# A gated linear recurrence with a two-layer MLP on one core: the order table of all five engines replaced

## The chip, the cores and the metric

The kernel runs on one core of a Trainium2 chip. The metric is device time in microseconds (us) of one execution, as a median over runs. The engines are named as in the profile: PE (TensorE; its weight loads are listed apart as PEld), DVE (VectorE), ACT (ScalarE), POOL (GpSimd) and SP (SyncE, which here only issues DMAs). PSUM has eight banks, which PE writes and DVE and ACT read.

## The reference, cut to what matters

```python
# q, k, v, a_re, a_im: (4, 8, 768, 48) = batch, heads, steps, head_dim
mag = sqrt(a_re*a_re + a_im*a_im)
scale = minimum(mag, 0.999) / (mag + 1e-6)
ar, ai = a_re*scale, a_im*scale
for t in range(768):                       # per batch and head; S is 48 x 48, complex
    S_re, S_im = ar*S_re - ai*S_im + outer(k[t], v[t]), ar*S_im + ai*S_re   # ar, ai at step t, by row of S
    y[t] = q[t] @ S_re
x = y with the heads side by side          # (4, 768, 384)
xn = (x - mean(x)) / sqrt(var(x) + 1e-6) * g_ln
out = x + maximum(xn @ w_ch1, 0) @ w_ch2   # 384 -> 1536 -> 384
```

A complex number a at each step and channel turns and shrinks the state; k times v is added; q reads the real part. A layer norm and an MLP with a residual follow.

## The kernel before

**Tiling.** The 768 steps of a batch are cut in chunks of 128. Two chunks make a *pair*, so there are 12 pairs P (0 to 11, three for each of the four batches) and 24 chunks n. Pair 0 is done in two halves of four heads each (names with .0 and .1 behind the pair number), all other pairs in one piece.

**The steps of a pair.** Loads a_re, a_im, q, k and v (tiles are, aim, q, k, vf; L449 and L408). ACT takes ln(a_re) (L452) and 1/a_re as Exp (L454); DVE or POOL form the ratio r = a_im/a_re; its square r2 is made by DVE, POOL or ACT (L462 on ACT), and ACT takes u = ln(1 + r2) (L466). DVE makes l = u/2 + ln(a_re) and caps it (the capped one is called lc). PE sums the log decays along the steps with a triangular matrix (dec, L481) and ACT makes from these sums e and en, their Exp with plus and minus sign (L485). ACT takes the angle th = arctan(r), PE sums it into phases (ph, L506 to L514; in turns, read as 16-bit integers), ACT reads sine and cosine from these (pairs 0 to 2 over a quarter turn that PE adds, qt; the others over an absolute value, abs, that ACT (L549) or DVE makes), and the last phase is carried to the next pair (car, on ACT L524, or DVE). Then the products: ke = k en, qe = q e (two halves each, m = 0 and 1), ks = ke times cosine and times sine, qs likewise (L293 is the helper line of all these products; the last digit of ks.P.i.a is 0 for the cosine, 1 for the sine). So each pair after pair 0 has two ks and two qs products, 128x768 each, on DVE or POOL.

**Attention.** For each chunk, ks and qs are transposed: on PE into PSUM (kT, qT, eight transposes each, L612) with a copy out by ACT (L288) or DVE (L290), the tiles ksT and qsT; or, with no PE work, by a DMA transpose on SP's queue (L617). am = ksT times qsT (L635), masked to atm by DVE; y = atm v + qsT G (L685, L688), copied to x by ACT or DVE; G is the state, from gm (L659, L663).

**MLP.** x is transposed by PE (xtr, L706) and copied to xT, or transposed by DMA (L712). mm1 multiplies by w1b (L740; 36 matmuls a pair, in three groups gi of two parts), relu goes to h (ACT L757 or DVE L759), and mm2 multiplies by w2b (L772; three parts for each chunk, part j needing the group j of h and the weight piece wl.3+j). bn makes mean and variance, rstd is 1/sqrt of the variance (POOL, L725 and L727; on ACT a Ln and an Exp, L722), oa and ot scale and add x (L778, L785, L788), st stores (L795). The weights come by six loads on POOL's queue: wl.0 to wl.2 fill w1b (L368), wl.3 to wl.5 fill w2b (L370). g_ln and the mean are folded into w1b at the start (wp, wc).

ACT holds one table set at a time. Ln and Exp need the one (tab.log), Arctan and Sin the other (tab.trig), and each change is a load on L810. In the start PE runs filler matmuls (warm, L805).

**What sets the order.** Nothing is scheduled while it runs or by the compiler: a text, PLAN (L39), lists every operation as *name:engine and PSUM bank*, and each engine's row is the order of its tokens in this text. Letters: P is PE, A ACT, V DVE, G POOL, S SP's queue. A DMA on A is issued from ACT's queue, in ACT's row. An '@' and a name behind a token is an added wait: this operation starts only after the named one, even though it doesn't use its result. All other waits follow from the data and from buffers: each tile has a ring of two to ten buffers, and a step that writes a buffer waits for the readers of what was in it.

```python
aim.0.0:A are.0.0:S pickf:V tab.log.0:A ln.0.0:A iv.0.0:A are.1.0:S gln:S ue:G cmean:G uth:V r.0.0:V are.0.1:S one:G
...
ke.7.0.0:G ks.7.0.0:G lc.8.0:V mm2.11.1:P6 mm2.11.2:P6 u.9.0:A ln.10.0:A y.12:P5 x.12:A5 mm2.10.1:P0 k.8.0:S l.9.0:V
```

A buffer's number in a row of an engine is the pair, or the chunk, modulo the ring: ks1 is ks of pair 1, 4, 7 or 10 (three buffers), ksT0 and ksT1 are ksT of chunks 20 and 21 in pair 10 (four buffers).

Of the kernel before, what the change touches and what calls it, by code (L numbers as in the profile page):

```python
# [69 lines left out]
ph.3.0:P0 atm.2:V4 car.3.0:V0 u.3.0:A xtr.3:P2 xT.3:V2 y.2:P6 x.2:A6 abs.3.0:V0 r.4.0:G mm1.0.2.0:P4 tab.trig.5:A  # L70
sin.3.0:A0 G.3:V7 xtr.2:P2 xT.2:V2 k.3.1:S are.6.0:S bn.2:V mm1.0.2.1:P4 mm1.1.1.0:P2 are.7.0:S mm1.1.2.1:P6
mm1.1.1.1:P2 bn.3:V cos.3.0:A relu.0.2:V4 bn.1:V pad.ks.2:G@ks.1.0.1 mm1.1.2.0:P6 relu.1.2:V6 mm1.1.0.1:P4 l.3.0:V
are.5.0:S ke.2.0.1:G@ks.1.0.1 ks.2.0.0:V th.4.0:A mm1.1.0.0:P4 mm2.0.0:P0 lc.3.0:V relu.1.1:A2 q.4.0:S qs.2.0.0:V
aim.6.0:S mm2.1.0:P3 mm2.1.1:P3 r2.4.0:G@ks.1.0.0 tab.log.6:A u.4.0:A ks.2.0.1:V vf.3.0:S aim.5.0:S relu.1.0:A4
l.4.0:V v.2:A rstd.1:A dec.3.0:P6 en.3.0:A6 k.4.0:S e.3.0:A6 mm2.0.1:P0 qs.2.0.1:V mm2.1.2:P3 kT.5:P5 kT.4:P1 rstd.0:G
vf.3.1:S q.5.1:S oa.1:A3 lc.4.0:V dec.4.0:P6 ksT.5:A5 qe.3.0.0:V qe.3.0.1:V qs.3.0.1:V en.4.0:A6 qs.3.0.0:V mm2.2.0:P2
mm2.0.2:P0 ot.0:V0 qT.4:P3 e.4.0:A6 mm2.2.1:P2 mm2.2.2:P2 qsT.4:V3 ke.3.0.1:G@qs.3.0.0 ln.6.0:A ke.3.0.0:V ks.3.0.1:G
k.4.1:S ph.4.0:P6 ln.5.0:A st.0:S iv.5.0:A iv.6.0:A ot.2:V2 ksT.4:V1 car.4.0:V6 ks.3.0.0:G@ke.3.0.0 dps.3:P4 qT.7:P2
qsT.7:A2 dps.4:P5 q.4.1:S decc.3:V4 r.6.0:G@ke.3.0.0 qT.5:P0 r.5.0:G@ke.3.0.0 r2.5.0:G decc.4:V5 abs.4.0:A6 qT.6:P3
q.5.0:S qsT.5:V0 am.4:P4 atm.4:V4 gm.4:P0 qsT.6:V3 tab.trig.7:A cos.4.0:A mm2.3.0:P1 kT.6:P2 G.4:A0 mm2.3.1:P1  # L80
v.3:G@ke.3.0.0 ksT.6:V2 am.5:P4 are.9.0:S k.5.0:S atm.5:V4 sin.4.0:A6 kT.7:P3 ksT.7:V3 y.4:P0 mm2.3.2:P1 vf.4.0:S
ot.3:V1 th.5.0:A x.4:A0 qe.4.0.0:G y.5:P5 x.5:V5 am.6:P6 ot.1:G atm.6:V6 qe.4.0.1:G@ke.3.0.0 th.6.0:A aim.7.0:S
vf.4.1:S am.7:P2 xtr.4:P1 k.6.0:S atm.7:V2 xT.4:A1 xtr.5:P0 xT.5:A0 ph.5.0:P4 abs.5.0:A4 sin.5.0:A4 gm.6:P0 cos.5.0:A
mm1.2.1.0:P6 G.6:V0 ke.4.0.1:G@qs.3.0.0 y.6:P1 x.6:V1 mm1.2.1.1:P6 relu.2.1:V6 y.7:P5 x.7:A5 bn.7:V xtr.6:P1
ke.4.0.0:G@qs.3.0.0 xT.6:A1 k.5.1:S mm1.2.2.0:P2 r2.6.0:A xtr.7:P5 xT.7:V5 ks.4.0.1:V q.6.0:S qs.4.0.1:V mm1.2.0.1:P6
mm1.2.0.0:P6 relu.2.0:V6 gm.7:P0 G.7:V0 mm1.3.0.1:P4 tab.log.8:A u.5.0:A l.5.0:V mm1.2.2.1:P2 relu.2.2:A2 mm1.3.0.0:P4
relu.3.0:A4 bn.5:V u.6.0:A lc.5.0:V are.8.0:S ks.4.0.0:G@qs.4.0.1 ksT.8:S mm1.3.1.0:P6 mm1.3.1.1:P6 mm1.3.2.1:P2
dec.5.0:P4 mm1.3.2.0:P2 relu.3.1:A6 v.4:V mm2.5.0:P6 qs.4.0.0:V qT.8:P7 l.6.0:V kT.9:P0 lc.6.0:V e.5.0:A4
qe.5.0.1:G@l.6.0 en.5.0:A4 dec.6.0:P4 bn.4:V relu.3.2:V2 ln.7.0:A ksT.9:V0 iv.7.0:A rstd.2:A en.6.0:A4 mm2.5.1:P6
# [5 lines left out]
xtr.9:P5 xT.9:A5 xtr.8:P1 xT.8:A1 aim.10.0:S rstd.3:G mm2.6.1:P0 ke.6.0.1:V ke.6.0.0:G mm2.6.2:P0 oa.7:A4 ph.7.0:P2
abs.7.0:A2 mm1.4.0.0:P6 sin.7.0:A2 car.7.0:A2 q.7.1:S ot.6:V0 ks.5.0.1:V ks.6.0.0:V mm1.4.1.1:P4 qsT.10:S mm1.4.1.0:P4
bn.8:V mm1.4.0.1:P6 qT.11:P1 relu.4.1:A4 tab.log.10:A ln.9.0:A qsT.11:V1 v.5:G@ks.5.0.1 mm1.4.2.1:P2 mm1.4.2.0:P2
relu.4.2:A2 dec.7.0:P4 en.7.0:A4 qs.6.0.1:G@ks.5.0.1 kT.11:P1 relu.4.0:V6 ot.7:G@lc.7.0 st.4:S e.7.0:A4 mm2.9.0:P7
# [743 lines left out]
```

## Time and profile before

| | |
|---|---|
| median of 3 runs | 190.76 us (189.49 to 191.31) |
| span of the profiled execution | 187.1 us |
| PE busy | 176.4 us, 94% |
| DVE busy | 153.7 us, 82% |
| ACT busy | 160.0 us, 86%, of it 24.4 in 19 table loads |
| POOL busy | 111.1 us, 59% |
| DMA moved | 37.39 MB, 200 GB/s in the mean |

The span runs from the first to the last instruction of the profiled execution; the runs' times hold what lies around it too. A row of a group names the line, the engine, the operation, the tiles (out <- in) with their shape, and the count; behind the bar stand the busy time and the mean of one in ns, and behind the next bar the idle time just ahead of these instructions on their engine with what ended it. A row of the chain of waits gives the start and the length of a stretch of the chain, in us from the span's start, and whose work it was. A row of the timeline gives start and length of one instruction, and in brackets the wait ahead of it with what ended it. A busy PE is not a PE at its best pace: its time holds short waits between matmuls too.

### The profile page before, as it was taken

The numbers are of one execution on the slowest core, as the hardware profiler recorded it, in microseconds if no ns is written. First come the engines' busy times: TensorE is split into PE (matmuls) and PEld (weight loads), VectorE is DVE, ScalarE is ACT, GpSimd is POOL, SyncE is SP. The second block draws the span as 40 slices with busy tenths as digits, with TensorE's granted clock in tenths as the row PEclk, the third lists the DMA queues.
The fourth block names the chain that finished last, engine by engine and source line by source line (L and its number), as shares of the span: only waits on it lengthen the run. The fifth ranks groups of instructions, "written<-read, shape, count | busy, mean of one in ns | idle before, by whom it ended". The sixth has DMA issues, their size and how long they took to land.

```text
span 187.1 us, 5110 instructions
## 1 busy us (share of the span) xinstructions
PE 176.4 (94%) x2025; PEld 135.1 (72%) x2027; DVE 153.7 (82%) x275; ACT 160.0 (86%) x228; POOL 111.1 (59%) x130
## 2 busy tenths in 40 slices
PE   5978898999999999999999999999999998999993
PEld 3756565787767789866687696878867866778772
DVE  1479999999989999999979989899879888866332
ACT  3889999999999989999999999998999897274560
POOL 3328699589207996288176692365879759420600
PEclk9999999999999999999999999999999999999999
DMA  5999999999999999699999997999999969996122
GB/s 148 291 256 227 223 260 189 207 206 194 233 261 239 219 221 191 128 203 309 204 155 238 256 265 92 185 247 169 216 175 215 203 144 229 210 199 173 40 90 84
DMA packets 132439, 37.39 MB, mean 200 GB/s; under 512 B 126528, under 2 KB 132416, under 8 KB 132416
## 3 DMA queue, kind: packets, MB, share of 16 engines
q1 hardware_dynamic: 123040, 32.45, 83.9%
q0 software_dynamic: 2784, 2.36, 8.2%
q10 hardware_dynamic: 6592, 2.26, 4.7%
q8 instruction: 16, 0.26, 0.6%
q14 instruction: 7, 0.06, 0.1%
HBM read 28.31 MB, written 4.72 MB: 177 GB/s over the span
## 4 chain that ended last, share of the span: by engine, by line
PE 71%; DVE 10%; DMA 6%; ACT 4%; POOL 3%; SPq 2%; issue 2%; DVEq 0%; POOLq 0%
PE banks L772 25%; PE banks L740 21%; PE banks L635 5%; PE banks L612 4%; PE banks L506 4%; PE banks L481 4%; DMA aim<-in_a_im_dram 3%; PE banks L685 2%; DMA qsT<-qs 2%; PE banks L706 2%; PE banks L688 2%; DMA are<-in_a_re_dram 2%; PE banks L663 2%; SPq L408 1%; DVE r L293 1%
## 5 line engine op out<-in xcount | busy, mean ns | idle before, releaser
L772 PE MATMUL banks<-w2b,h 128*128 128x384 bf16 (+1 forms) x300 | 53.8, 319 | 0.0
L740 PE MATMUL banks<-xT,w1b 128*128 128x256 bf16 x432 | 51.4, 272 | 0.2 <-DVE xT L290 0.2
L740 PEld LDWEIGHTS <-w1b 128*128 128x128 bf16 x432 | 41.3, 98 | 6.3 <-issue 0.4
L772 PEld LDWEIGHTS <-h 128*128 128x128 bf16 x300 | 27.1, 97 | 13.3
L293 DVE TENSOR_TENSOR atm<-banks,mask 128x1024 bf16<-128x1024 f32 x24 | 28.8, 1219 | 5.1 <-PE banks L635 5.0
L757 ACT ACTIVATE h<-banks 128x1024 bf16<-128x1024 f32 (+1 forms) x24 | 23.8, 1003 | 5.3 <-PE banks L740 5.1
L293 POOL TENSOR_TENSOR qe<-q,e 128x384 bf16<-128x384 f32 x19 | 17.5, 929 | 15.7 <-ACT e L485 9.1
L810 ACT ACT_TABLE_LOAD x19 | 24.4, 1283 | 1.7 <-PEq L826 1.3
L293 POOL TENSOR_TENSOR ke<-k,en 128x384 bf16<-128x384 f32 x16 | 14.8, 939 | 7.5 <-DVE qs L293 6.8
L759 DVE TENSOR_SCALAR h<-banks 128x1024 bf16<-128x1024 f32 (+1 forms) x13 | 15.2, 1169 | 3.6 <-PE banks L740 3.6
L805 PE MATMUL banks<-u_e 128*128 128x256 f16 x111 | 15.5, 297 | 2.2 <-POOL u_e L322 2.2
L635 PE MATMUL banks<-qsT,ksT 128*128 128x128 bf16 x192 | 14.1, 219 | 1.0 <-DMA qsT<-qs 0.7
L805 PEld LDWEIGHTS <-u_e 128*128 128x128 f16 x111 | 11.5, 106 | 4.5 <-POOL u_e L322 1.9
L293 POOL TENSOR_TENSOR r<-aim,are 128x768 f16<-128x768 f32 x7 | 12.6, 1811 | 3.0 <-ACT are L454 3.0
L635 PEld LDWEIGHTS <-ksT 128*128 128x128 bf16 x192 | 11.9, 98 | 2.5 <-issue 1.1
L293 POOL TENSOR_TENSOR qs<-qe,trig 128x768 bf16<-128x768 bf16 (+1 forms) x8 | 12.6, 1576 | 1.6 <-DVE qe L293 0.9
L470 DVE SCALAR_TENSOR_TENSOR l<-r,w 128x768 f16<-128x768 f16 (+1 forms) x13 | 12.3, 949 | 1.3 <-ACT r L466 1.1
L785 POOL TENSOR_TENSOR ot<-ot,x 128x384 f32<-128x384 f32 x11 | 10.5, 966 | 4.6 <-ACT ot L778 4.3
L698 DVE BATCH_NORM_STATS2 stats<-x 128x6 f32<-128x384 bf16 x24 | 13.1, 548 | 0.0
L288 ACT CAST x<-banks 128x384 bf16<-128x384 f32 x19 | 8.8, 478 | 5.0 <-PE banks L688 4.5
L293 POOL TENSOR_TENSOR ks<-ke,trig 128x768 bf16<-128x768 bf16 (+1 forms) x7 | 10.7, 1539 | 2.8 <-DVE qs L293 1.6
L685 PE MATMUL banks<-v,atm 128*128 128x48 bf16 x192 | 11.9, 183 | 0.0
(101 smaller groups left out, 380.4 us busy)
## 6 DMA issues: line engine op xcount, KB each, us to landing
q<-in_q_dram SPq DMA_DIRECT2D x24, 192.0 KB, 4.7
k<-in_k_dram SPq DMA_DIRECT2D x24, 192.0 KB, 4.5
...
```

The source lines that it names most:

```text
L293: {"DVE": nc.vector, "POOL": nc.gpsimd}[eng(name)].tensor_tensor(**kw)
L470: nc.vector.scalar_tensor_tensor(out=S_("l"), in0=S_("r2"), scalar=0.5, in1=S_("w"), op0=ALU.mult, op1=ALU.add)
L635: nc.tensor.matmul(ps[:, h], lhsT=T("ksT", n)[:, h], rhs=T("qsT", n)[:, h], start=True, stop=True)
L685: nc.tensor.matmul(ps[:, h], lhsT=T("atm", n)[:, h], rhs=T("v", P)[:, c, h], start=True, stop=nfirst)
L698: nc.vector.bn_stats(out=T("stats", n), in_=T("x", n))
L740: nc.tensor.matmul(ps[:, jj], lhsT=w1b[:, dc, ts(gi * JG + jj, C)], rhs=T("xT", P)[:, dc].rearrange("p c t -> p (c t)"), start=(dc == 0), ...
L757: act(out=dst, in_=src, func=AF.Relu)
L759: nc.vector.tensor_scalar(out=dst, in0=src, scalar1=0.0, scalar2=None, op0=ALU.max)
L772: nc.tensor.matmul(bank(own)[:, 0:w], lhsT=T("h", P)[:, j, ts(c, C)], rhs=w2b[:, j, es], start=(j == 0), stop=(j == NJ - 1))
L785: nc.gpsimd.tensor_tensor(out=T("ot", n)[:, es], in0=T("ot", n)[:, es], in1=T("x", n)[:, es], op=ALU.add)
L805: g.add(f"warm.{i}", lambda i=i: nc.tensor.matmul(bank(f"warm.{i}")[:, 0:256], lhsT=u_e[:, 0, 0], rhs=u_e[:, 1].rearrange("p j t -> p (j t ...
L810: g.add(f"tab.{nm}.{i}", lambda tab=tab: nc.scalar.preload_act_table_set(tab))
```

## The change

Only the text PLAN differs. The same operations are computed, 1,137 tokens where there were 1,136: one table load less on ACT (tab.log.18, the 19th), and two more groups of eight PE transposes, kT.10 and qT.17, since ksT.10 and qsT.17 were DMA transposes on SP and are now copied out of PSUM, by DVE and by ACT. DMA transposes that remain: 11 of ks, 11 of qs and 1 of x, where there were 12, 12 and 1. All five rows have a new order, many PSUM banks are renumbered, and there are 51 added waits where there were 49.

Steps that change engine, counted over the whole program:

| step | moves |
|---|---|
| ks | 10 from DVE to POOL, 3 from POOL to DVE |
| qs | 4 and 4 |
| ke, qe | ke 3 DVE to POOL, 4 back; qe 4 DVE to POOL, 7 back |
| abs, car | 3 and 4 from DVE to ACT |
| x, xT | x 8 from ACT to DVE, 1 back; xT 11 from ACT to DVE, 4 back |
| ksT, qsT copies | ksT 1 ACT to DVE, 1 DVE to ACT; qsT 3 DVE to ACT, 2 ACT to DVE |
| relu, G, r | relu 4 ACT to DVE, 5 back; G 3 and 3; r 1 and 1 |
| r2 | both halves of pair 0 and 3 pairs from ACT to DVE, 1 DVE to ACT, and 4 moves from or to POOL |
| rstd | 4 ACT to POOL, 2 POOL to ACT |
| v | one each from POOL to ACT and to DVE, 2 from DVE to POOL |
| DMA issues | vf 5 and a_im 1 from ACT's queue to SP's, q 1 back; stores 6 from ACT's to SP's, 4 back |

The first and a late piece of the table, as the diff has them:

```diff
-aim.0.0:A are.0.0:S pickf:V tab.log.0:A ln.0.0:A iv.0.0:A are.1.0:S gln:S ue:G cmean:G uth:V r.0.0:V are.0.1:S one:G
+are.0.1:S tab.log.0:A ue:G aim.0.1:S uth:V warm.0:P0 warm.1:P0 warm.2:P0 are.0.0:S ln.0.1:A are.1.0:S car0.1:G
+aim.0.0:S warm.3:P0 iv.0.1:A warm.4:P0 r.0.1:V warm.5:P0 ln.0.0:A warm.6:P0 aim.1.0:S pad.ks.0:G iv.0.0:A r2.0.1:V
```

SP's row begins with a_re and a_im of pair 0's second half, a_re of its first half and of pair 1, a_im of the first half and of pair 1, and k of pair 0; before, it began with a_re of the first half, of pair 1 and of the second half, a_im of the second half (that of the first half was ACT's to issue) and q of pair 0.

The weight load wl.5 stood right behind wl.4 on POOL; it now stands behind r.4 and waits for DVE's lc.3 (wl.5:G@lc.3.0). In the change of tables ahead of pair 3's phases, xT.2 stands behind the load on ACT now. Of the vf loads, vf.6.0 stands on SP behind the DMA transpose qsT.12. Of the twelve ks and qs products of pairs 9, 10 and 11, POOL has eight (three with a wait on a relu or an xT), where it had four. Both stores of the last chunk are issued by SP, where one was ACT's.

ACT, from its first table load on: before, w0, are0 and r20 are pair 0 (two halves), w1, are1 and r21 pair 1; L462 is a Square, L466 the Ln behind it, L485 an Exp of the decay sums.

```order
L810 ACT_TABLE_LOAD
L452 ACTIVATE w0_82<-are0_64 128x384
L454 ACTIVATE are0_64<-w0_82 128x384
L462 ACTIVATE r20_87<-r0_84 128x384
L466 ACTIVATE r20_87<-r20_87 128x384
L452 ACTIVATE w1_83<-are1_65 128x768
L452 ACTIVATE w0_82<-are0_64 128x384
L454 ACTIVATE are0_64<-w0_82 128x384
L454 ACTIVATE are1_65<-w1_83 128x768
L462 ACTIVATE r20_87<-r0_84 128x384
L466 ACTIVATE r20_87<-r20_87 128x384
L466 ACTIVATE r21_88<-r21_88 128x768
```

The same place after.

```order
L810 ACT_TABLE_LOAD
L452 ACTIVATE w0_82<-are0_64 128x384
L454 ACTIVATE are0_64<-w0_82 128x384
L452 ACTIVATE w0_82<-are0_64 128x384
L454 ACTIVATE are0_64<-w0_82 128x384
L466 ACTIVATE r20_87<-r20_87 128x384
L452 ACTIVATE w1_83<-are1_65 128x768
L454 ACTIVATE are1_65<-w1_83 128x768
L466 ACTIVATE r20_87<-r20_87 128x384
L485 ACTIVATE e0_97<-banks_63 128x2x192
L462 ACTIVATE r21_88<-r1_85 128x768
L466 ACTIVATE r21_88<-r21_88 128x768
```

Both half Squares of pair 0 left the row and pair 1's came in; Ln and Exp of both halves stand together ahead of the first u.

POOL around pair 7: before, qe1, ke1, ks1 and qs1 are pair 7's, v2 is v of pair 6, ot2 and ot4 are the outputs of chunks 7 and 9, r0 is the ratio of pair 9.

```order
L293 TENSOR_TENSOR r0_84<-aim0_67,are0_64 128x768
L293 TENSOR_TENSOR qe1_109<-q1_71,e1_98 128x384 x2
L418 TENSOR_SCALAR v2_80<-vf0_76 128x768
L785 TENSOR_TENSOR ot4_166<-ot4_166,x9_141 128x384
L293 TENSOR_TENSOR qs1_114<-qe1_109,trig1_102 128x16x48
L293 TENSOR_TENSOR ke1_107<-k1_74,en1_100 128x384
L293 TENSOR_TENSOR ks1_111<-ke1_107,trig1_102 128x16x48 x2
```

The same place after; rstd0 is that of pair 5 and r21 the square of pair 9.

```order
L293 TENSOR_TENSOR r0_84<-aim0_67,are0_64 128x768
L293 TENSOR_TENSOR qe1_109<-q1_71,e1_98 128x384
L293 TENSOR_TENSOR ke1_107<-k1_74,en1_100 128x384 x2
L293 TENSOR_TENSOR qs1_114<-qe1_109,trig1_102 128x16x48
L293 TENSOR_TENSOR r21_88<-r0_84 128x768
L785 TENSOR_TENSOR ot2_164<-ot2_164,x7_139 128x384
L418 TENSOR_SCALAR v2_80<-vf0_76 128x768
L293 TENSOR_TENSOR ks1_111<-ke1_107,trig1_102 128x16x48 x2
L725 TENSOR_SCALAR rstd0_151<-mv0_146 128x2
L727 TENSOR_TENSOR rstd0_151<-rstd0_151,half_n_175 128x2
L293 TENSOR_TENSOR qs1_114<-qe1_109,trig1_102 128x16x48
L785 TENSOR_TENSOR ot4_166<-ot4_166,x9_141 128x384
```

All four products ks and qs of pair 7 are here now, the first qs ahead and the second behind both ks and an rstd; the first of the two ks has an added wait, for DVE's relu.5.0 (ks.7.0.1:G@relu.5.0).

SP around the transposes of pair 10 (ks1 and qs1; ksT0 and qsT0 are chunk 20, ksT1 and qsT1 chunk 21): before, q2 and vf1 are loads of pair 11, x8 is x of chunk 18.

```order
L712 DMA_TRANSPOSE xT1_157<-x8_140 128x3x128
L617 DMA_TRANSPOSE ksT1_117<-ks1_111 128x8x128
L408 DMA q2_72<-in_q_dram 128x8x48
L617 DMA_TRANSPOSE ksT0_116<-ks1_111 128x8x128
L617 DMA_TRANSPOSE qsT1_121<-qs1_114 128x8x128
L617 DMA_TRANSPOSE qsT0_120<-qs1_114 128x8x128
```

The same place after.

```order
L617 DMA_TRANSPOSE ksT1_117<-ks1_111 128x8x128
L712 DMA_TRANSPOSE xT1_157<-x8_140 128x3x128
L408 DMA q2_72<-in_q_dram 128x8x48
L617 DMA_TRANSPOSE qsT1_121<-qs1_114 128x8x128
L617 DMA_TRANSPOSE qsT0_120<-qs1_114 128x8x128
L617 DMA_TRANSPOSE ksT0_116<-ks1_111 128x8x128
L408 DMA vf1_77<-in_v_dram 128x8x48 x2
```

The order was ksT.21, ksT.20, qsT.21, qsT.20 and is now ksT.21, qsT.21, qsT.20, ksT.20.

More of the change, by code (lines that the diff above doesn't have):

```diff
@@ L70 @@
[L70 to L89, printed above, removed]
@@ L95 @@
[L95 to L98, printed above, removed]
-mm2.8.0:P6 bn.9:V rstd.4:G mm2.9.1:P7 ksT.11:V1 am.11:P2 iv.9.0:A r.9.0:G gm.10:P0 G.10:A0 ks.6.0.1:V r.8.0:V
@@ new lines @@
+e.5.0:A4 mm2.5.1:P6 ke.5.0.0:V v.4:G@ke.5.0.0 st.0:S qsT.8:V7 dec.6.0:P4 st.2:S relu.3.2:A2 ln.8.0:A bn.6:V en.6.0:A4
+q.6.1:S mm2.4.0:P7 qe.5.0.1:G@bn.6 bn.7:V am.8:P2 rstd.3:A mm2.4.1:P7 ksT.9:V1 gm.8:P1 st.1:S mm2.4.2:P7 e.6.0:A4
+atm.8:V2 vf.5.1:S qe.5.0.0:G y.8:P0 G.8:V1 k.7.0:S iv.8.0:A r.7.0:G gm.9:P1 ke.6.0.1:G@G.8 mm2.5.2:P6 ph.6.0:P2
+qs.5.0.1:V am.9:P4 r2.7.0:A G.9:V1 ke.5.0.1:G u.7.0:A q.7.1:S qs.5.0.0:V mm2.7.0:P1 x.8:V0 mm2.6.0:P0 abs.6.0:A2
+tab.trig.9:A atm.9:V4 ks.5.0.1:G@x.8 mm2.6.1:P0 qT.11:P4 ot.4:V7 q.7.0:S are.9.0:S v.5:V ot.5:V6 sin.6.0:A2 y.9:P5
@@ new lines @@
+bn.8:V k.9.0:S kT.11:P1 kT.13:P4 ksT.10:V0 dec.7.0:P6 ksT.11:V1 e.7.0:A6 am.11:P0 vf.6.1:S en.7.0:A6 qsT.12:S
+mm2.9.0:P3 mm2.9.1:P3 vf.7.0:S ksT.13:V4 mm2.8.0:P6 rstd.4:A q.9.0:S atm.11:V0 am.10:P0 atm.10:V0 qe.7.0.1:V
+tab.trig.11:A kT.12:P5 ksT.12:A5 vf.6.0:S mm2.9.2:P3 mm2.8.1:P6 th.8.0:A y.10:P1 qsT.13:S y.11:P0 cos.7.0:A x.10:V1
+r.9.0:G oa.9:A3 x.11:V0 qe.7.0.0:G ke.7.0.1:G th.9.0:A ph.8.0:P4 xtr.10:P2 ke.7.0.0:G@x.10 xtr.11:P3 q.8.1:S xT.11:V3
+qs.7.0.0:G mm2.8.2:P6 abs.8.0:A4 r2.9.0:G@x.11 sin.8.0:A4 ph.9.0:P0 xT.10:V2 are.10.0:S mm1.5.0.0:P2 bn.11:V
@@ new lines @@
+sin.9.0:A0 ot.8:V6 mm1.5.0.1:P2 car.9.0:A0 mm1.5.1.0:P6 ot.7:G abs.9.0:A0 v.6:G am.12:P4 bn.10:V r2.8.0:A cos.8.0:A
+relu.5.0:V2 mm1.5.1.1:P6 atm.12:V4 tab.log.12:A ks.7.0.1:G@relu.5.0 relu.5.1:V6 k.8.1:S mm1.5.2.1:P2 are.11.0:S
+dps.7:P1 am.13:P4 ks.7.0.0:G mm2.10.0:P0 atm.13:V4 decc.7:V1 u.8.0:A gm.12:P7 y.12:P6 l.8.0:V rstd.5:G G.12:A7 x.12:A6
+lc.8.0:V mm1.5.2.0:P2 relu.5.2:A2 st.7:S gm.13:P7 st.8:S dps.6:P5 decc.6:V5 xtr.12:P4 y.13:P1 k.8.0:S x.13:V1
+mm2.10.1:P0 dec.8.0:P2 v.7:V mm2.11.0:P6 xtr.13:P5 ln.10.0:A q.8.0:A aim.10.0:S u.9.0:A mm2.11.1:P6 xT.13:V5 xT.12:A4
@@ new lines @@
+qe.9.0.0:G@r.10.0 q.10.1:S atm.16:V2 mm2.14.1:P7 gm.16:P3 th.10.0:A tab.log.14:A y.16:P2 relu.7.2:A0 x.16:A2 G.16:V3
+st.9:S vf.10.1:S am.17:P5 dec.10.0:P0 atm.17:V5 xtr.16:P3 xT.16:V3 mm2.14.2:P7 u.11.0:A ot.11:G e.10.0:A0 y.17:P4
+ph.10.0:P2 q.10.0:S qs.9.0.1:G@decc.9 en.10.0:A0 ke.10.0.0:G@xT.16 x.17:A4 qs.9.0.0:V ksT.18:S st.10:S bn.17:V
+dps.10:P5 decc.10:V5 qsT.18:S qsT.19:S mm2.15.0:P6 xtr.17:P4 st.11:S tab.trig.15:A xT.17:V4 ke.10.0.1:V mm2.15.1:P6
+mm1.8.1.0:P4 sin.10.0:A2 l.11.0:V rstd.7:G@xT.17 mm2.15.2:P6 mm1.8.0.0:P0 qe.10.0.1:V lc.11.0:V v.9:A mm1.8.1.1:P4
@@ new lines @@
+xT.19:V3 tab.trig.17:A G.19:V7 ke.11.0.0:V ot.16:V1 ke.11.0.1:V qsT.21:S mm2.17.2:P0 ph.11.0:P4 qsT.20:S
+qe.11.0.0:G@x.19 ot.14:G@ke.11.0.0 mm1.9.1.0:P6 abs.11.0:A4 mm1.9.1.1:P6 relu.9.1:V6 mm1.9.2.0:P1 sin.11.0:A4
+mm1.9.0.1:P3 oa.17:A0 mm1.9.0.0:P3 gm.20:P0 G.20:V0 cos.11.0:A ks.11.0.0:G qe.11.0.1:G am.21:P5 atm.21:V5 ksT.20:S
+relu.9.0:A3 mm1.9.2.1:P1 vf.11.0:S vf.11.1:S relu.9.2:A1 mm2.19.0:P3 rstd.9:G@atm.21 gm.21:P0 mm2.19.1:P3 am.20:P6
+qs.11.0.0:V mm2.18.0:P4 y.21:P2 x.21:A2 mm2.19.2:P3 ks.11.0.1:G@ke.11.0.0 v.11:G qs.11.0.1:V atm.20:V6 st.14:S G.21:V0
@@ L142 @@
+mm1.11.0.0:P4 bn.23:V mm1.11.0.1:P4 oa.20:A7 ot.20:G@x.23 mm1.11.1.0:P2 relu.11.2.1:V0 mm1.11.1.1:P2 oa.21:A6
+mm1.11.2.0:P0 bn.22:V st.20:S ot.18:G@atm.22 relu.11.0:A4 st.18:S mm2.22.0:P5 relu.11.1:V2 mm2.23.0.1:P4 mm2.22.1:P5
+rstd.11:G relu.11.2.0:A0 ot.21:G mm2.22.2:P5 ot.22:V5 mm2.23.1.1:P4 mm2.23.0.0:P0 st.21:A mm2.23.2.1:P4 ot.23.1:V4
+mm2.23.1.0:P0 mm2.23.2.0:P0 st.23.1:S ot.23.0:V0 st.22:A st.23.0:S
 """
```

147 lines of the change are left out of this document (71 added, 76 removed).

## The prediction

> **What bounds the kernel now.** I read the page first, then the stretches, PE's waits, the chain of waits, and the rows of ACT, POOL and SP at the places that the change touches. In the three stretches below the columns are the length, then the busy time of PE, its weight loads, DVE, ACT and POOL with their instructions, the granted clock, DMA share and GB/s.
>
> ```profile
> span 187.1 us, 5110 instructions
> 45.00:60.00 15.00, 14.93 (x144) 10.92 (x144) 14.13 (x30) 14.90 (x22) 5.66 (x7) 1.00 1.08 237
> 60.00:75.00 15.00, 14.86 (x221) 12.45 (x218) 14.58 (x23) 14.09 (x20) 13.04 (x11) 1.00 0.97 213
> 90.00:105.00 15.00, 15.00 (x172) 11.15 (x171) 12.86 (x23) 14.90 (x21) 7.47 (x8) 1.00 1.09 207
> PE banks L635 <- DMA qsT<-qs: 0.7, 1, 0.7
> PE banks L740 <- DVE xT L290: 0.2, 1, 0.2
> ```
>
> From 45 us on PE has no hole, and the last two rows are all that its matmuls wait for between 36 and 184 us. ACT is as full: 43.9 of the 45 us in these stretches, 1.1 us of waiting. So I count PE's useful work (all but the filler on L805) at the pace at which the chain of waits passes it, and call *lag* the time at a point of PE's row less the useful work that stands ahead of it.
>
> ```profile
> 72.77 3.93 PE banks L740 x36
> 80.20 2.60 PE banks L772 x16
> 53.06 0.89 PE banks L612 x16
> 123.68 0.89 PE banks L635 x16
> 51.11 0.65 PE banks L481 x4
> 57.74 1.02 PE banks L506 x6
> 68.08 0.20 PE banks L663 x8
> 45.07 4.09 PE banks L740 x36
> 117.80 0.45 PE banks L612 x8
> 183.93 0.42 DVE ot L788
> ```
>
> A matmul costs 0.109 us on L740, 0.1625 on L772, 0.056 on L612 and L635. 432 on L740 are 47.2; 276 full and 24 half ones on L772 46.9; 192 and 192 on L612 and L635 21.4; the decay sums on L481 7.8; the phase sums on L506 and L510/L514 12.2; y on L685/L688 (352 as narrow as L663's, 0.025) 9.0; the state products 5.3; 69 x transposes at L612's pace 3.9; the few left (dps, wp, qt), by their column counts, 4.3. Together 158.0 us. The last product ends at 183.9: lag 25.9. Ahead of the 45.07 row stand 21.7 us (36 of L740, 96 of L612 and L635, five groups of decay and of phase sums, four each of y, state product and x transposes, 3.3 of the few): lag 23.4. Ahead of the 117.80 row stand 93.4: lag 24.4. So the kernel is 158.0 of work, 23.4 lost in the start, 1.0 in the middle, 1.5 late (0.7 of it the wait for qsT), and 3.2 after the last product. The profiled execution's span is 187.1; the median of the runs shown, 190.76, is 3.7 more, which I add at the end unchanged.
>
> **The change, part by part.** *PE* gets kT.10 and qT.17, 16 transposes, 0.9 us of useful work: 158.9. Nobody waited for the two DMA transposes that go, so nothing comes back for them.
>
> *Start.* Here ACT sets the pace.
>
> ```profile
> 5.84 0.52 ACT L462 ACTIVATE r<-r 128x384 f16<-128x384 f16 x1 [0.62 <-DVE r L293]
> 10.97 0.84 ACT L466 ACTIVATE r<-r 128x768 f16<-128x768 f16 x1 [0.65 <-DVE r L293]
> 17.12 1.28 ACT L810 ACT_TABLE_LOAD   x1
> 43.82 1.28 ACT L810 ACT_TABLE_LOAD   x1
> 110.50 1.28 ACT L810 ACT_TABLE_LOAD   x1
> ```
>
> The first piece lands as before, being the first load on SP again. Both half Squares of pair 0 leave ACT (2 x 0.52) and one full Square comes (0.84): -0.2. The wait of 0.62 was for DVE's r; now the other half's Ln and Exp stand there, and what can be late is that half's a_re, third on SP, for which I keep 0.5. The wait of 0.65 was for pair 1's Square on DVE; ACT now makes it itself, with u.0.0 and e.0.1 to do until r.1.0 is there: some 0.2 stays. So the load at 17.12 comes near 16.6. From it to the load at 43.82 ACT loses x.1, x.2 and qsT.2 and gains a half car, a Square (r2.3) and G.2.
>
> ```profile
> L549 ACT ACTIVATE sh<-banks 128x768 f16<-128x768 int16 x6 | 4.9, 809 | 0.5 <-PE banks L506 0.4
> L524 ACT ACTIVATE car<-banks 32x384 f16<-32x384 int16 x3 | 1.4, 483 | 0.3 <-PE banks L506 0.2
> L288 ACT CAST x<-banks 128x384 bf16<-128x384 f32 x19 | 8.8, 478 | 5.0 <-PE banks L688 4.5
> L288 ACT COPY xT<-banks 128x384 bf16<-128x384 bf16 x13 | 5.8, 481 | 0.9 <-PE banks L706 0.5
> L288 ACT COPY qsT<-banks 128x1024 bf16<-128x1024 bf16 x2 | 2.0, 1020 | 0.0
> L722 ACT ACTIVATE rstd<-mv 128x2 f32<-128x2 f32 x5 | 1.0, 205 | 0.4 <-DVE mv L699 0.2
> L727 POOL TENSOR_TENSOR rstd<-rstd,half_n 128x2 f32<-128x2 f32 x7 | 5.0, 710 | 0.6
> L725 POOL TENSOR_SCALAR rstd<-mv 128x2 f32<-128x2 f32 x7 | 2.5, 351 | 12.3 <-DVE mv L699 10.2 <-DVE l L473 2.0
> L293 POOL TENSOR_TENSOR ks<-ke,trig 128x768 bf16<-128x768 bf16 x6 | 9.7, 1636 | 2.7 <-DVE qs L293 1.6 <-DVE ke L293 1.0
> L293 DVE TENSOR_TENSOR ks<-ke,trig 128x768 bf16<-128x768 bf16 x16 | 8.6, 550 | 0.2
> L759 DVE TENSOR_SCALAR h<-banks 128x1024 bf16<-128x1024 f32 x12 | 14.5, 1209 | 0.6 <-PE banks L740 0.6
> ```
>
> That is -0.48 - 0.48 - 1.02 + 0.3 + 0.84 + 0.48 (G.2 by x, of one shape) = -0.4, so the load comes near 42.9 (bounds: 42.0, if the waits go, and 44.3, if the start's loads come late). xT.2 now stands behind it on ACT: 42.9 + 1.28 + 0.48 = 44.7; ACT's copies start a little before the one ahead ends, so I take 44.4. The other inputs of pair 1's first product on L740 are due by then. Its lag is 44.4 - 21.7 = 22.7, where before had 23.4.
>
> *Middle.* Between the loads at 43.82 and 110.50 ACT's row gains two Abs (1.62), three car (1.45), a qsT copy (1.02) and an rstd of two such steps (0.41), and loses two xT (0.96) and one x (0.48); relu, G, ksT and Squares come out even: +3.1 us. At the rate of 1.1 in 45, some 1.5 us of waiting stand between the two loads to take it in. 42.9 + 66.7 + 3.1 - 1.5 puts the load at 111.2, 0.7 later than before. Behind it comes G.12, which PE needs at 89.1 us of work: 111.2 + 1.28 + 0.84 (u) + 0.48 - 0.3 (overlap) = 113.5, lag 24.4. What the start gained is spent by here. Bounds: 22.7, if PE needs ACT's new work only late, and 25.0, if none of the waits go. I take 24.4, because ACT's row is full.
>
> DVE gives ten ks to POOL and takes three back, loses Abs and car to ACT and takes x and xT from it, some 4 us less in all; it has 0.4 to 2.1 us of room in each stretch, and I cost it at nothing. That room is the cover; without it an x or xT is late by its own half us. POOL takes a net seven ks (7 x 1.64) and about 1 us of smaller pieces.
>
> *Late.* The DMA transposes of chunks 20 and 21 set PE's wait of 0.7.
>
> ```profile
> 141.54 1.54 POOL L418 TENSOR_SCALAR v<-vf 128x768 bf16<-128x768 f32 x1
> L418 POOL TENSOR_SCALAR v<-vf 128x768 bf16<-128x768 f32 x7 | 6.7, 962 | 7.3 <-issue 4.7 <-DMA vf<-in_v_dram 2.5
> 148.69 1.89 POOL L293 TENSOR_TENSOR qs<-qe,trig 128x768 bf16<-128x768 bf16 x1 [0.94 <-DVE qe L293]
> 151.31 1.23 SPq L617 DMA_TRANSPOSE ksT<-ks  x1
> 154.88 3.19 SPq L617 DMA_TRANSPOSE qsT<-qs  x2
> 159.01 0.61 PE L635 MATMUL banks<-qsT,ksT 128*128 128x128 bf16 x8 [0.71 <-DMA qsT<-qs]
> DMA to landing us min/median/max: 3.9/3.9/4.0
> L370 POOL DMA_DIRECT2D w2b<-in_moe_w_ch_dram x3: 747/811/811, 36.2 to 39.5; - x3
> ```
>
> In SP's row both qsT stood behind both ksT; now ksT.20 stands last, so qsT.21 goes when qs.10 is ready. That product starts on POOL near 149.4 now, behind one more ks of its pair, and ends near 151; qsT.21 lands by 156 and am.21 finds it. I take the 0.7 as gone and a quarter of the other 0.8 as staying: lag 24.6 at the end.
>
> Seven DMA issues go from ACT's queue to SP's, whose row is in order: vf.6.0 now stands behind qsT.12, which waits for POOL's qs.6.0.1, but v.6 is due some 3 us after it lands. The sixth weight load (wl.5, last of the three in the last row) is moved past r.4 on POOL and waits for DVE's lc.3, which follows relu.0.2: near 44.2 + 1.2 and a half us, 46, where before it was issued at 39.5. By the 6.4 to 9.6 us that the three took to land, it lands between 52.4 and 55.6. Its first reader, mm2.1.2, stands at 30.6 us of work, due at 53.3: a wait of 0 to 2.3. Up to 1.7 of it is free, since the middle reaches lag 24.4 in any case. I take nothing, and keep 0.6 for the range.
>
> The end is the same six products, with both last stores on SP, the second due some 0.5 us after the first: no change. Sum: 158.9 + 24.6 = 183.5; + 3.2 = 186.7 of span; + 3.7 = 190.4 us.
>
> A rule against the change: POOL's 1.54 for v (mean 0.96) and 1.89 for qs (ks of its shape 1.64) lie beside DVE work, so each can stretch. The Trainium skill, SBUF — State Buffer, section Who interferes with whom, says that a DVE operation with two SBUF inputs and a GpSimd operation that reads SBUF exclude each other, the later one blocking. By it seven ks that each meet one DVE product cost 7 x 0.55 = 3.9 us, 194.3 if all of it reached PE; by the stretches seen they cost POOL about 7 x 0.25 = 1.8, which its idle time takes in. The trace agrees in kind.
>
> **Rivals.** *Slower: POOL becomes the chain.* For pair 7 all four products ks and qs are POOL's. ks.7.0.1 waits for DVE's relu.5.0 to end, then come ks, ks, rstd and qs: 1.2 + 1.64 + 1.64 + 1.1 + 1.64 = 7.2 us from the end of mm1.5.0 to qs.7.0.1, and PE reaches qT.15 8.5 us of work after it. The margin is 1.3 us, two stretches like the 0.6 of v. From there each us of POOL is a us of PE. Pairs 9 to 11, with eight of twelve such products on POOL where before had four, repeat it: 1 us lost at each of three places makes lag 27.6 and 193.4 us. For it: 12 us more on POOL, and the stretches. Against it: POOL idles 2 to 9 us in each stretch above.
>
> *Faster: ACT's +3.1 finds room.* If PE needs Abs, car and qsT late, and x and xT, which leave ACT, were what tied it to PE, the lag of 22.7 lasts, with 0.3 lost late: 158.9 + 23.0 + 3.2 + 3.7 = 188.8. For it: x and xT lie directly in PE's chain. Against it: ACT's full rows.
>
> *The start's loads come late*, since pair 0's a_im and k stand ahead of q on the one queue: +1.0 to 1.5 that passes through, 191.4 to 191.9.
>
> **How the numbers follow.** Forecast 0.45 (190.4; its own range 189.3 to 191.6, from the middle's bounds and w2b), POOL 0.25, ACT 0.22, loads 0.08. A measurement can tell about 1% from no change: below 188.85 or above 192.7. ACT's case lies on the bound with its larger part beyond it, and the forecast's spread adds some: faster 0.24. POOL's case with what is worse than the loads' case: slower 0.28. Same 0.48. The range leaves out ACT's best outcomes and POOL late at more than three places: 188.1 to 193.4.
>
> **What would show it.** Right, if ACT's second load stands near 16.6, its load ahead of pair 3's phases near 42.9, pair 1's first product on L740 near 44.4, the load at 110.50 near 111 with ACT still above 14.5 of 15, and no wait for qsT near 159. Wrong, if PE waits for ks or qs of POOL or for w2b, if ACT idles over 2 us between 45 and 105, or if the start's lag is outside 22 to 24.

## The result, and the profile after

The changed kernel takes 196.2 us in the median of 4 runs (195.15 to 196.76); the kernel before, run again beside it, 191.03 (189.49 to 192.38). The ratio is 1.029, interval 1.022 to 1.035: slower, by 5.2 us. The two profiled executions lie further apart, 195.1 against 187.1: the one of after is the longest of its four (193.4 to 195.1), and the one of before is shorter than all its later runs, which have spans of 187.6 to 190.7, each 1.9 to 2.1 below its time. The ratios given here leave out executions that were disturbed (over 1.5% above the fastest of their kernel), the medians don't; where they disagree both are told.

The page's first line and the three stretches, with the columns of before:

```profile
span 195.1 us, 5157 instructions
45.00:60.00 15.00, 13.58 (x124) 10.20 (x124) 14.44 (x23) 14.21 (x19) 9.01 (x9) 1.00 1.07 203
60.00:75.00 15.00, 14.15 (x215) 10.91 (x212) 13.66 (x22) 14.36 (x24) 14.29 (x12) 1.00 1.03 216
90.00:105.00 15.00, 14.74 (x158) 10.98 (x158) 14.32 (x26) 14.81 (x20) 10.96 (x8) 1.00 0.78 171
```

PE has holes now, 2.3 us in the first two stretches, where before had 0.2. ACT is about as full as before (43.4 of 45 for 43.9), and POOL has 34.3 for 26.2.

What PE's matmuls waited for behind 36 us (the table of waits: who was waited for, us, times, the longest; three further rows have 0.3 or less):

```profile
PE banks L740 <- ACT xT L288: 1.5, 1, 1.5
PE banks L612 <- DVE h L759: 1.4, 1, 1.4
PE banks L706 <- DVE x L290: 1.0, 1, 1.0
```

No wait for a DMA transpose of qs stands there any more. The lag, counted as in the prediction (158.9 of useful work now):

| place | before | forecast | after |
|---|---|---|---|
| first decay sum | 7.9 | | 8.8 |
| first product on L740 of pair 1 | 23.4 | 22.7 | 25.5 |
| ahead of 58 us | 23.4 | | 27.1 |
| ahead of 78 us | 24.0 | | 28.8 |
| first product on L740 of pair 6 | 24.2 | 24.4 | 31.8 |
| last transposes of x (chunk 23) | 25.7 | 24.6 | 32.6 |

Of the 6.9 us that the lag grew, 2.1 come in the start and 4.2 at three places: 1.4 near 55 us, 1.2 near 75 and 1.6 near 125. The other rows differ by 0.6 in all. With the 0.9 of added PE work and 0.2 behind the last product these make the 8.0 between the two spans. The rows of the three places and of the start follow in the order of the program.

*The start.* PE's timeline, and its granted clock (the third figure from the right) in slices of 1 us:

```profile
2.22 4.00 PE L805 MATMUL banks<-u_e 128*128 128x256 f16 x18 [2.22 <-POOL u_e L322]
8.76 0.49 PE L481 MATMUL banks<-l,u_e 128*128 128x192 f16 x4 [2.54 <-DVE l L473]
9.09 5.00 PE L805 MATMUL banks<-u_e 128*128 128x256 f16 x29
13.92 0.49 PE L481 MATMUL banks<-l,u_e 128*128 128x192 f16 x4
...
9.00:10.00 1.00, 1.00 (x11) 0.86 (x9) 0.79 (x1) 0.91 (x3) 0.90 (x3) 0.80 0.95 251
10.00:11.00 1.00, 1.00 (x7) 0.69 (x6) 0.89 (x4) 0.80 (x1) 0.86 (x4) 0.50 1.07 239
11.00:12.00 1.00, 1.00 (x7) 0.69 (x6) 0.40 (x3) 0.97 (x3) 0.24 (x1) 0.50 1.05 248
```

The kernel before has 32 fillers ahead of the first decay sum and 22 between the two halves; its row of the latter:

```profile
8.19 2.56 PE L805 MATMUL banks<-u_e 128*128 128x256 f16 x22
11.75 0.49 PE L481 MATMUL banks<-l,u_e 128*128 128x192 f16 x4 [1.00 <-DVE l L473]
```

With 18 ahead PE idles for 2.54 us, and the 29 between the halves then take 0.17 each instead of 0.12. DVE had the second half's l ready at 11.4; its sum waited behind the fillers until 13.92. ACT's rows behind it, the Exp of that sum, 1/a_re and the table load, moved with it.

*Near 55 and 75 us.* Two rows of DVE with the rows of POOL at the same time:

```profile
51.34 2.80 DVE L293 TENSOR_TENSOR ks<-ke,trig 128x768 bf16<-128x768 bf16 x1
72.66 1.97 DVE L293 TENSOR_TENSOR r<-r 128x768 f16<-128x768 f16 x1
...
50.65 1.48 POOL L293 TENSOR_TENSOR r<-r 128x768 f16<-128x768 f16 x1
52.08 1.64 POOL L293 TENSOR_TENSOR ks<-ke,trig 128x768 bf16<-128x768 bf16 x1
72.57 1.64 POOL L293 TENSOR_TENSOR ks<-ke,trig 128x768 bf16<-128x768 bf16 x1
```

DVE's ks, 0.55 in the mean before, ends at 54.14, when POOL's two operations are done (53.72) and its own half us has passed. The square, which takes 0.56 elsewhere in this trace, ends at 74.63, behind POOL's ks (74.21). Behind the first stand a relu, behind the second x of chunk 7: PE's waits of 1.4 and 1.0.

*Near 125 us.* ACT's rows, POOL's and PE's:

```profile
120.30 3.42 ACTq L408 DMA_DIRECT2D q<-in_q_dram  x1
120.37 0.85 ACT L452 ACTIVATE w<-are 128x768 f32<-128x768 f32 x1
123.78 0.84 ACT L466 ACTIVATE r<-r 128x768 f16<-128x768 f16 x1 [2.55 <-POOL ot L785]
124.52 0.46 ACT L288 COPY xT<-banks 128x384 bf16<-128x384 bf16 x1
...
120.80 1.63 POOL L293 TENSOR_TENSOR qs<-qe,trig 128x768 bf16<-128x768 bf16 x1
...
125.04 2.23 PE L740 MATMUL banks<-xT,w1b 128*128 128x256 bf16 x18 [1.45 <-ACT xT L288]
```

PE waits for ACT's xT, and ACT idled 2.55 us ahead of it. The table puts that down to POOL's ot of pair 4, and the chain of waits goes on from there through POOL's whole chain of pair 7, as my first rival had it. But the L466 needs only POOL's square, done at 114.2. Meanwhile ACT's queue has the issue of a load, q of pair 8, that lasts until 123.72. The two readings have to be told apart by a run.

### The profile page after: what moved, and what is told of

It is laid out like the page before. It is cut to its first block, busy times and chain, and to the rows that moved or that the text cites. A ratio compares the mean times of both kernels' runs of the same rounds, so it can differ in the third digit from the quotient of the medians.

```text
span 195.1 us, 5157 instructions
## 1 busy us (share of the span) xinstructions
PE 178.8 (92%) x2043; PEld 137.0 (70%) x2043; DVE 159.8 (82%) x274; ACT 161.0 (83%) x221; POOL 126.8 (65%) x139
## 4 chain that ended last, share of the span: by engine, by line
PE 53%; DVE 20%; ACT 10%; POOL 7%; issue 4%; DMA 3%; SPq 1%; DVEq 0%; POOLq 0%
PE banks L772 17%; PE banks L740 14%; PE banks L635 4%; PE banks L612 3%; DVE ks L293 3%; PE banks L481 3%; PE banks L506 3%; DMA aim<-in_a_im_dram 3%; PE banks L805 2%; DVE h L759 2%; DVE atm L293 2%; DVE w1b L392 2%; ACT L810 2%; POOL qs L293 2%; POOL ks L293 2%
## 5 line engine op out<-in xcount | busy, mean ns | idle before, releaser
L772 PE MATMUL banks<-w2b,h 128*128 128x384 bf16 (+1 forms) x300 | 55.5, 319 | 0.0
L740 PE MATMUL banks<-xT,w1b 128*128 128x256 bf16 x432 | 51.4, 272 | 1.5 <-ACT xT L288 1.5
L740 PEld LDWEIGHTS <-w1b 128*128 128x128 bf16 x432 | 41.5, 98 | 7.6 <-issue 1.6
L293 POOL TENSOR_TENSOR ks<-ke,trig 128x768 bf16<-128x768 bf16 (+1 forms) x14 | 22.2, 1594 | 11.3 <-issue 3.0
L757 ACT ACTIVATE h<-banks 128x1024 bf16<-128x1024 f32 (+1 forms) x25 | 24.7, 1008 | 5.6 <-PE banks L740 5.5
L293 POOL TENSOR_TENSOR ke<-k,en 128x384 bf16<-128x384 f32 x17 | 17.0, 1009 | 7.0 <-ACT en L485 4.6
L805 PE MATMUL banks<-u_e 128*128 128x256 f16 x111 | 18.4, 317 | 2.4 <-POOL u_e L322 2.2
L293 POOL TENSOR_TENSOR qe<-q,e 128x384 bf16<-128x384 f32 x16 | 15.1, 949 | 2.8 <-ACT e L485 1.0
L759 DVE TENSOR_SCALAR h<-banks 128x1024 bf16<-128x1024 f32 (+1 forms) x12 | 14.1, 1174 | 3.0 <-PE banks L740 2.9
L293 POOL TENSOR_TENSOR qs<-qe,trig 128x768 bf16<-128x768 bf16 x8 | 13.1, 1634 | 1.1 <-DVE qe L293 1.0
L466 ACT ACTIVATE r<-r 128x768 f16<-128x768 f16 (+1 forms) x13 | 10.3, 793 | 2.6 <-POOL ot L785 2.5
L452 ACT ACTIVATE w<-are 128x768 f32<-128x768 f32 (+1 forms) x13 | 10.2, 796 | 2.7 <-DMA are<-in_a_re_dram 2.7
## 6 DMA issues: line engine op xcount, KB each, us to landing
k<-in_k_dram SPq DMA_DIRECT2D x24, 192.0 KB, 4.3
vf<-in_v_dram SPq DMA_DIRECT2D x24, 192.0 KB, 4.0
q<-in_q_dram SPq DMA_DIRECT2D x23, 192.0 KB, 4.3
out_dram<-ot SPq DMA_DIRECT2D x19, 192.0 KB, 3.4
```

Source lines behind the costliest of these rows:

```text
L293: {"DVE": nc.vector, "POOL": nc.gpsimd}[eng(name)].tensor_tensor(**kw)
L466: add(f"u.{X}", lambda S_=S_: act(out=S_("r2"), in_=S_("r2"), func=AF.Ln, bias=1.0), needs=[f"r2.{X}"], uses=[("r2", P)])
L740: nc.tensor.matmul(ps[:, jj], lhsT=w1b[:, dc, ts(gi * JG + jj, C)], rhs=T("xT", P)[:, dc].rearrange("p c t -> p (c t)"), start=(dc == 0), ...
L757: act(out=dst, in_=src, func=AF.Relu)
L759: nc.vector.tensor_scalar(out=dst, in0=src, scalar1=0.0, scalar2=None, op0=ALU.max)
L772: nc.tensor.matmul(bank(own)[:, 0:w], lhsT=T("h", P)[:, j, ts(c, C)], rhs=w2b[:, j, es], start=(j == 0), stop=(j == NJ - 1))
```

## The experiments

All are the changed kernel with something undone, except where named; ratios are to the kernel before.

**The load q of pair 8 on SP's queue.**

```diff
-q.8.0:A
+q.8.0:S
```

> The changed kernel with one DMA issue, the load q of pair 8's first chunk, back on SP's queue from ACT's. Theory of separate places: the 3.42 us that this issue takes on ACT at 120.3 makes PE's wait of 1.45 us for xT ahead of pair 6's first product on L740; without it that wait is gone, the span is 193.4 to 194.0 instead of 195.1, and the time 194.5 to 195.1, 1.020 to 1.024 of the kernel before. Rival, POOL's chain of pair 7 (its qs ends at 122.43): ACT still waits near 121 to 123 and PE near 123 to 125, span 195, no change.

194.12 us, ratio 1.018 (1.013 to 1.022). ACT's row at the place:

```profile
119.03 0.85 ACT L452 ACTIVATE w<-are 128x768 f32<-128x768 f32 x1
119.76 0.85 ACT L466 ACTIVATE r<-r 128x768 f16<-128x768 f16 x1
120.50 0.49 ACT L288 COPY xT<-banks 128x384 bf16<-128x384 bf16 x1
```

The L466 runs without a wait, and PE's 1.5 is gone, while POOL works as before: its ot ends at 122.28, 2.5 us after the L466 has begun. So it was the issue, and POOL's chain was a wrong attribution. The span of 192.4 is lower than forecast for a second reason, since in this execution the start was better: pair 1's first product on L740 stands at 45.91 us, lag 24.1, where the changed kernel had 47.28 and 25.5.

**A second load on ACT's queue, early.** Why should an issue take 3.42 us, where all of before on ACT's queue took 0.34 to 0.68? It was the queue's first in the changed kernel. (On SP's queue long issues stand in the kernel before too, 4.20 us for an a_re at 17.10.)

```diff
-vf.0.0:S
+vf.0.0:A
```

> The changed kernel with a second load on ACT's queue, v of pair 0's first chunk near 13 us, so that q of pair 8 is no longer the first DMA of that queue. Theory of the first use: its issue takes 0.35 to 0.5 us instead of 1.8 to 3.8, and the early one takes the long time instead. Rival, the issue waits for what the memory or SP's transposes do near 118 to 122: it takes 1.8 us or more again.

194.76 us, in a single execution. The two issues of ACT's queue:

```profile
10.83 0.43 ACTq L408 DMA_DIRECT2D vf<-in_v_dram  x1
120.07 0.39 ACTq L408 DMA_DIRECT2D q<-in_q_dram  x1
```

The late issue is short now and PE's wait is gone; but the early one is short too, so half of the expectation fell. As the first of its queue q took 3.42, 3.84, 1.78, 1.93, 3.74 and 1.45 us in six kernels. PE waited for the xT behind it (1.5, 1.9 and 1.8 us) in the three with over 3 us, and not in the others. Why a first issue at 10 us costs nothing and one at 120 does was not found, and that being the first is the cause rests on this one execution.

**Two turns at the port.** A turn is an added wait: POOL's operation starts only when DVE's beside it has ended, so that the two don't meet.

```diff
-r2.4.0:G
+r2.4.0:G@ks.2.0.0
-ks.4.0.1:G@atm.5
+ks.4.0.1:G@r2.5.0
```

> The changed kernel with two added waits: POOL's square of pair 4 behind DVE's ks.2.0.0, and POOL's ks.4.0.1 behind DVE's square of pair 5. Theory of the shared port: DVE's ks at 51.3 (2.80 us) and its square at 72.7 (1.97) are held until POOL's operation beside them ends; with the turns both fall to 0.55, PE's waits of 1.4 (near 55) and 1.0 (near 75) go, the span is 192.6 to 193.4 and the time 193.8 to 194.5, 1.015 to 1.020. Rival, DVE's row is full whatever the turns: the two operations shorten, but POOL's delayed work or the next DVE step makes PE wait instead, span above 194.6.

192.93 us in the median of 11 runs, ratio 1.005 (1.000 to 1.010; by the medians 1.009): 3.3 us less than 196.2, more than the 1.7 to 2.4 expected. DVE's ks and its square:

```profile
51.53 0.53 DVE L293 TENSOR_TENSOR ks<-ke,trig 128x768 bf16<-128x768 bf16 x1
72.16 0.53 DVE L293 TENSOR_TENSOR r<-r 128x768 f16<-128x768 f16 x1
```

Neither is held, and both waits of PE are gone; a wait of 0.9 for the weights w2b has come. From pair 1's first product on L740 to pair 3's it takes 29.1 us, where the changed kernel takes 31.1. So the trace shows 2.0 of the 3.3; the rest isn't accounted for. The profiled execution took 196.81 us in all: its start was as late as that of the changed kernel, the issue of q took 3.84, and PE waited 1.3 for a DMA transpose of ks, a wait that the changed kernel's trace doesn't have.

**The first turn alone.**

```diff
-r2.4.0:G
+r2.4.0:G@ks.2.0.0
```

> The changed kernel with the first of the two turns alone (POOL's square of pair 4 behind DVE's ks.2.0.0). Theory of separate places: ks.2.0.0 falls from 2.80 to 0.55, PE's wait of 1.4 for DVE's relu near 55 goes or falls under 0.5, while the square at 72.7 is still held near 2.0 and PE's wait of 1.0 for x stays. Rival, one fullness of DVE: the wait near 75 goes too, or another of 1 us takes the place of the first.

195.25 us, in a single execution; the start was long in it (the second half's sum at 14.85). DVE's two rows, and PE near 58:

```profile
52.28 0.53 DVE L293 TENSOR_TENSOR ks<-ke,trig 128x768 bf16<-128x768 bf16 x1
72.87 1.97 DVE L293 TENSOR_TENSOR r<-r 128x768 f16<-128x768 f16 x1
...
58.00 0.81 PE L772 MATMUL banks<-w2b,h 128*128 128x384 bf16 x4 [0.71 <-DMA w2b<-in_moe_w_ch_dram]
```

Each place stands by itself: the ks is short, the square is still held, and PE's 1.0 for x stays. The wait of 1.4 is gone, and half of it comes back as a wait for w2b, the sixth weight load. In the changed kernel that load is issued at 49.82 and nobody waits for it: the held ks had covered it.

**Fewer fillers between the halves.**

```diff
-warm.18:P0 ... warm.31:P0
```

> The changed kernel without 14 of the 29 filler matmuls that stand in PE's row between the two halves of pair 0's decay sums. It computes the same; only filler is gone. Theory that the fillers stand in the way: the second of the two sums starts near 11.7 instead of 13.9, ACT's load ahead of the phases near 16.5 instead of 18.3, and the lag at pair 1's first product falls by 1.4 to 2, span 193.1 to 193.7. Rival, DVE's row bounds the start: the sum starts earlier, but the lag at that product falls by under 0.5, span 194.6 to 195.1.

193.66 us, ratio 1.013 (1.009 to 1.017). The sum starts at 11.96, ACT's load at 16.53, and the lag at pair 1's first product is 23.4: the start is that of the kernel before. The span of 191.2 is 2 us below the forecast because the issue of q took only 1.78 in this execution and PE did not wait for xT; so the 2.5 us that the median fell can't be put down to the start alone.

**The same fillers in front.** The 14 tokens now stand ahead of the first half's sum.

```diff
+warm.18:P0 ... warm.31:P0
 dec.0.1:P6
-warm.18:P0 ... warm.31:P0
```

> The changed kernel with the same 14 fillers not dropped but moved ahead of the first half's decay sums, where the kernel before had them (32 ahead, 15 between). Theory that PE's 2.5 us of idling makes the fillers behind it slow: without the gap they run at 0.12 each as in the kernel before, the second half's sum starts near 11.5, and the time is that of the run without these 14 (193.7) or up to 0.5 less. Rival, their number alone counts: each still takes 0.17 to 0.2, the sum starts near 12, and PE's row in the first 30 us looks as in that run, time 193.4 to 194.

193.5 us, ratio 1.012 (1.006 to 1.018).

```profile
8.78 0.49 PE L481 MATMUL banks<-l,u_e 128*128 128x192 f16 x4 [0.40 <-DVE l L473]
9.11 1.80 PE L805 MATMUL banks<-u_e 128*128 128x256 f16 x15
11.37 0.49 PE L481 MATMUL banks<-l,u_e 128*128 128x192 f16 x4 [0.46 <-DVE l L473]
```

With a gap of 0.40 each filler takes 0.12, and the second sum waits for DVE again, not for fillers. In the run without them the gap was 2.58 and 15 fillers took 3.36 us, 0.22 each.

**The kernel before with 14 fillers moved behind the first sum.**

```diff
-warm.18:P0 ... warm.31:P0
 dec.0.0:P6
+warm.18:P0 ... warm.31:P0
```

> The kernel before with one thing of the change: 14 of the 32 fillers ahead of the first half's decay sums moved behind them. Theory: PE idles near 5 to 7.8 us, the 36 fillers between the sums run slowly, the second sum starts near 14 instead of 11.75, and the time is 1.5 to 2.5 us longer, 1.008 to 1.013. Rival, the gap costs nothing since ACT sets the pace of the start: under 0.5 us, 1.000 to 1.003.

191.35 us in the median of 12 runs, ratio 0.996 (0.991 to 1.001): the theory failed here.

```profile
7.68 0.49 PE L481 MATMUL banks<-l,u_e 128*128 128x192 f16 x4 [1.87 <-DVE l L473]
8.00 4.09 PE L805 MATMUL banks<-u_e 128*128 128x256 f16 x36
11.93 0.49 PE L481 MATMUL banks<-l,u_e 128*128 128x192 f16 x4
```

After a gap of 1.87 us the 36 fillers run at 0.11 each, and the sum comes only 0.2 later. (A load of q that landed late holds POOL until 23.09 and then PE for 1.8 us in this execution; nothing shows that the fillers have a part in it.) So it isn't the move that costs. Behind gaps of 1.94, 2.23, 2.24, 2.30, 2.54, 2.58 and 2.73 us in the changed kernel and its other versions they took 0.16 to 0.22 each. The changed kernel's first sum comes later, because DVE's r of the other half, which waits for a_im, stands between l and its cap; that makes its gap longer.

**All three repairs together.** q on SP, the two turns, the 14 fillers in front.

> The changed kernel with the three repairs together: q of pair 8 on SP's queue, the two turns at the port, the 14 fillers in front. Theory of separate places: the gains add (2.1 + 3.3 + 2.5 by the medians so far) as far as no other wait takes their place; 189.0 to 191.0 us, 0.990 to 1.002 of the kernel before, with PE waiting for under 1 us behind 36 us. Rival, the rows of ACT and DVE are full and give only what one of the repairs gives: 192.5 to 194.

191.47 us in the median of 12 runs (190.6 to 191.83), ratio 1.0005 (0.997 to 1.004): 0.5 above the times expected and 1.0 below the rival's. PE waits for 1.5 us behind 36 us, not for under 1; 0.8 of it stands near 55 us, where DVE is late. ACT's three table loads that the forecast rests on, and the ks:

```profile
16.29 1.28 ACT L810 ACT_TABLE_LOAD   x1
42.78 1.28 ACT L810 ACT_TABLE_LOAD   x1
111.97 1.28 ACT L810 ACT_TABLE_LOAD   x1
...
48.67 0.52 DVE L293 TENSOR_TENSOR ks<-ke,trig 128x768 bf16<-128x768 bf16 x1
```

In the changed kernel these loads start at 18.34, 45.45 and 116.68. Pair 1's first product on L740 stands at 44.61, where 44.4 was forecast. The lag ends at 26.2, 6.4 less than there. The three single gains, 2.1 + 3.3 + 2.7 by medians of different sessions, are 8.1; the three together take off 4.7, which ends at the time of the kernel before (191.41) and not below it. One reason stands in the traces: the issue of q was short by itself in executions of other versions, so that a single gain can hold part of another. The rest is open.

**The two transposes back on SP**, in the changed kernel and then with the three repairs.

```diff
-kT.10:P0 ksT.10:V0 qT.17:P7 qsT.17:A7
+ksT.10:S qsT.17:S
```

> The changed kernel with the two transposes of chunks 10 and 17 back on SP as DMA transposes, the 16 PE transposes and the two copies out of PSUM gone. The term as it was forecast: 0.9 us of PE work and nothing else, span 194.2, time 195.3. Rival: PE waits for the DMA transposes, about 3.5 us from issue to landing, and it is no faster or up to 1 us slower.

196.17 us, ratio 1.024 (1.019 to 1.029): no faster, as the rival had it, though PE waits only 0.2 us for a DMA transpose.

> The kernel with the three repairs, and the transposes of chunks 10 and 17 back on SP. Theory that 16 PE transposes are 0.9 us of the path once no other wait hides them: 190.4 to 190.9 us, 0.994 to 0.998 of the kernel before. Rival: PE waits for the DMA transposes, or DVE and ACT don't use the room, 191.3 to 192.

192.0 us in the median of 12 runs, ratio 1.003 (0.999 to 1.006), the rival's time. PE waits for no DMA transpose, so 0.9 us less of PE's work shortened nothing: with the repairs the lag ends at 27.1 instead of 26.2, and the last product ends at 185.2 in both. PE's work doesn't set the time there. Which row does, ACT's or DVE's, was not tested.

**The kernel before with ksT of chunk 20 last on SP.**

```diff
-ksT.20:S qsT.21:S ... qsT.20:S
+qsT.21:S ... qsT.20:S ksT.20:S
```

> The kernel before with one part of the change: on SP, ksT of chunk 20 behind both qsT of pair 10. The forecast's late step: PE's wait of 0.7 us for qsT near 159 goes and the time is 0.5 to 0.8 us shorter, 0.996 to 0.998. Rival: the next wait takes its place (ksT of chunk 20, 3.8 us from issue to landing, or the next transposes), under 0.3 us.

PE's wait for qsT is gone from the trace, and the lag ends at 25.1 instead of 25.7. The time can't tell: the median of 6 runs is 191.42, for 191.29 of the kernel before, and the ratio of 0.990 (0.983 to 0.996) rests on the two lowest of the six.

No version beat the kernel before clearly.

## Why the prediction was wrong

The forecast was 190.4 us and no change; it is 196.2. Point by point:

- *DVE "I cost at nothing"; ks moved to POOL cost POOL about 1.8, "which its idle time takes in".* This step failed worst. The prediction put the stretch on POOL, but DVE paid. After, DVE's rows of ks are

```profile
L293 DVE TENSOR_TENSOR ks<-ke,trig 128x768 bf16<-128x768 bf16 x9 | 9.0, 1000 | 0.1
```

  1.00 each for 0.55: nine products cost more than the sixteen of before (9.0 us for 8.6). The Trainium skill (SBUF — State Buffer, Who interferes with whom) says that issue order decides which of the two blocks. In this trace operations of 1.6 us on POOL met ones of 0.55 on DVE, and it was DVE that stood still: 2.80 beside two of them, 1.97 beside one. I had cited the rule and priced it from the wrong side. Two such meetings stood ahead of a relu and an x that PE needed, 2.6 us of lag; the run with turns gave back 2.0 in its trace, net of the new wait for w2b, and 3.3 by the medians.
- *The start: ACT's second load near 16.6, lag 22.7.* The sum held ACT's own steps and left the filler out as not useful work. But a filler stands in PE's row: 29 of them at 0.17 held a sum on which ACT waited, 1.7 us at the load (18.34). With the fillers in front the load stands at 16.60, and with all repairs at 16.29: ACT's steps were right, the row ahead of them was missing. Rival three, late loads, was not it: a_im does come late, yet with the fillers in front ACT's load is not late.
- *"Seven DMA issues go from ACT's queue to SP's".* I followed those and not the one that came the other way. It cost 1.6 us of lag, by an effect that the trace of before doesn't show.
- *The middle: the load behind 42.9 near 111.2, lag 24.4.* With the repairs 42.78 and 111.97, so ACT's +3.1 less its waiting was mis-sized by 0.9 at most. (The lower end of the forecast's own range, 189.3, doesn't follow from the middle's bound of 22.7, which gives 188.7; nothing else hangs on it.) Without them the load is at 116.68: 2.7 of the difference stand at the load ahead, from the start, and 2.0 between the two, where both held operations lie.
- *POOL becomes the chain of pair 7, margin 1.3.* It did not: qs ends at 122.43 and its transposes start at 122.97, a margin of 0.5, and with q on SP nobody waits there.
- *Late: the wait for qsT goes.* Right, in the changed kernel and in the kernel before with that part alone; worth 0.6 of lag, too little for the time to show.
- *wl.5: "I take nothing", 0 to 2.3.* 0 in the changed kernel, 0.7 and 0.9 once its cover is taken away.
- *PE +0.9.* Not on the path: taking it away gained nothing in two pairs of runs.
- *+3.7 from span to time, unchanged.* 2.0 of it is what lies around the span; the rest is that the span shown is shorter than those of the runs. For the changed kernel 1.7 lies around it. By luck this hid over 2 us of the error: the span was missed by 8.4 us, the time by 5.8.
